# Start of a fused attention and mixer kernel: first constants and loads dealt anew to two DMA queues, with half a warming matmul less

## The chip, the cores and the metric

One core of a Trainium2 chip runs the kernel. The metric is the device time of one execution in microseconds (us). The kernel before was timed three times: 271.75, 270.02 and 270.61 us, median 270.61 us.

The engines go by their short names: PE (TensorE matmuls) and PEld (its weight loads), DVE (VectorE), ACT (ScalarE), POOL (GpSimd), SP (SyncE). A small q behind a name (SPq, ACTq) means the engine's instruction queue at work, for instance issuing a DMA.

## The reference

Four batches, eight heads, 768 positions, head size 64. Scores are masked by blocks of 32 positions: a block pair counts if it lies next to the diagonal, in the first or last block row or column, or if it was sampled for its row. Then softmax, the product with v, and a mixer over the result.

```python
scores = scale * np.matmul(q, k.transpose(0, 1, 3, 2))
mask = np.abs(blk_i - blk_j) <= window
mask = mask | (blk_i == 0) | (blk_j == 0) | (blk_i == n_blocks - 1) | (blk_j == n_blocks - 1)
for qb in range(n_blocks):
    for kb in sampled_blocks[qb]:
        mask[qb * block:(qb + 1) * block, kb * block:(kb + 1) * block] = True
attn = softmax(np.where(mask, scores, -1e9))
x = np.matmul(attn, v)                     # heads side by side: 4 x 768 x 512
h = x.transpose(0, 2, 1) @ U @ V           # low rank over the positions
u = x + h.transpose(0, 2, 1)
out = u + np.maximum(u @ w_ch1, 0.0) @ w_ch2
```

## The kernel before, in words

Heads are worked on in pairs, 16 in all. For each pair q and k are loaded with positions on the partitions, cast to fp16 and turned by PE, so that the head's 64 features lie on the partitions. In the first four pairs (batch 0) the mask goes into the score matmul itself. A head takes 64 partitions for its features and 24 more for the mask: in q's tile these rows hold a one-hot code of the position's block, in k's tile a bias of 0 or -240 for each block. One matmul then gives score plus bias, ACT takes the exponential, and PE multiplies by v. For later pairs a 0/1 mask is built once (L939, L945) and multiplied in by DVE.

All engines follow an order written out by hand (a word list called PLAN, and ahead of it the start, L243 to L342). Nothing is reordered at run time, so an instruction that waits holds up whatever stands behind it on its engine. DMAs are issued from SP's and ACT's queue. Each takes one of eight semaphores in turn, so a DMA waits until the one eight before it has landed.

The start, which is all that the change touches:

- `first_load(h, n, queue)` (L176, issue at L182) loads head h of pair 0: q for n = 0, k for n = 1. Head 0 comes first. Head 1, the second head, is issued later at the same line.
- `small` (L102 to L105, L245) is one constant for all 128 partitions: the static mask and block numbers `ms` and `iota` (24 rows), and the fp16 identity `id16` that PE needs for every turn.
- `sb` (L246) holds the sampled blocks. From `sb`, `iota` and `ms` DVE works out the bias (L302, L306, L309).
- `one_hot` (L186) loads the 24 one-hot rows into the q tile of a head, `qres[i][mrows[h], h]`. For the first set of tiles (i = 0) it is called twice at L254, each time behind a DVE memset (L253). For the second set (i = 1, used from pair 1 on) it is called in `second_set` (L192).
- `keep_warm(8)` (L300) gives PE eight matmuls of 512 columns on constants while it waits for data.
- Then `first_cast` (L213, DVE: fp32 to fp16), `first_turn` (L227, PE: three matmuls each), `first_row` (L293, copies out of the accumulators by ACT and DVE), `mask_half` (L279, PE: bias times one-hot rows) and `mask_row` (L287).
- The second heads of pair 0 are cast by POOL (L213) and turned by PE at L352, after the first scores (L980, L999). Their rows are copied by DVE at L359.
- `load_v(0)`, `load_qk(1)`, `load_v(1)` (L166, L153) follow on SP's queue, then U (L200), `second_set` (with the copy of the mask rows into `kmask`, L196) and V (L206).

The order of the first turn, which both kernels share but for line numbers (two more in the changed one):

```python
first_cast(0, 0, nc.vector.tensor_copy)     # L301
... neq, a01, bias on DVE ...
first_turn(0, 0)                            # L314
first_row(0, 0, nc.scalar.copy)
first_turn(0, 1)
first_row(0, 1, nc.scalar.copy)
first_cast(0, 1, nc.vector.tensor_copy)
mask_half(0)                                # L319
mask_row(0, 0, nc.vector.tensor_copy, 0, P)
mask_row(1, 0, nc.scalar.copy)
first_turn(1, 0)
```

Of the kernel before, what the change touches and what calls it, by code (L numbers as in the profile page):

```python
# [12 lines left out]
FP32 = mybir.dt.float32  # L13
FP16 = mybir.dt.float16
# [5 lines left out]
P = 128  # L20
# [3 lines left out]
def kernel(  # L24
# [14 lines left out]
    nc = tc.nc  # L39

    B, H, S, D = q.shape
    BLK = 32
    NB = S // BLK
# [9 lines left out]
    MASK_BIAS = -240.0  # L53
# [3 lines left out]
    ii = np.arange(NB)  # L57
    ms_np = (
        (np.abs(ii[None, :] - ii[:, None]) <= 1)
        | (ii[None, :] == 0)  # L60
        | (ii[:, None] == 0)
        | (ii[None, :] == NB - 1)
        | (ii[:, None] == NB - 1)
    ).astype(np.float32)
    cols = np.arange(S)
    blk = ((cols % P) * T + cols // P) // BLK
    ohT_np = (blk[None, :] == ii[:, None]).astype(np.float16)
    small_np = np.zeros((P, NB + 1 + P // 2), np.float32)
    small_np[:NB, :NB] = (ms_np - 1.0) * -MASK_BIAS
    small_np[:NB, NB] = ii  # L70
    small_np[:, NB + 1 :] = np.eye(P, dtype=np.float16).view(np.float32)

    small_dr = nc.inline_tensor(small_np, name="small_const")
    ohT_dr = nc.inline_tensor(ohT_np, name="one_hot_const")

    consts = ctx.enter_context(tc.tile_pool(name="consts", bufs=1))
    wpool = ctx.enter_context(tc.tile_pool(name="wpool", bufs=1))
# [21 lines left out]
        ring["psc"] += 1  # L99
        return PS[:, (0, 3)[ring["psc"] % 2] :][:, 0:2]  # L100

    small = consts.tile([P, NB + 1 + P // 2], FP32)  # L102
    ms = small[0:NB, 0:NB]
    iota = small[0:NB, NB : NB + 1]
    id16 = small[:, NB + 1 :].bitcast(FP16)  # L105
    sb = consts.tile([P, NB, 3, 2], I32)
    vts = [consts.tile([P, H, T, DV], FP16, name=f"vt{i}") for i in range(2)]
    NEST = 16
# [3 lines left out]
    res = consts.tile([P, 4, 2, S], FP16, name="res")  # L112
    qres = [res[:, i] for i in range(2)]
    kres = [res[:, 2 + i] for i in range(2)]
    drows = [slice(0, D), slice(D, P)]
    mrows = [slice(D, D + NB), slice(0, NB)]
    hid = consts.tile([P, 2, 16, HS], FP16, name="hid")
# [58 lines left out]
    def first_load(h, n, queue):  # L176

        src, nm = ((q, "qld"), (k, "kld"))[n]
        if h == 0:
            lds[nm] = ldpool.tile([P, 2, T, D], FP32, tag="ld" + nm, name=nm)  # L180
            sts[0, nm] = stpool.tile([P, T, 2, D], FP16, tag="st" + nm, name="st" + nm)
        queue.dma_start(  # L182
            out=lds[nm][:, h], in_=src[0, h].rearrange("(p t) d -> p t d", t=T)
        )

    def one_hot(i, h):  # L186
        nc.sync.dma_start(out=qres[i][mrows[h], h, :], in_=ohT_dr.ap())

    warm = nc.const_aps.tensor(1.0, [P, 512], mybir.dt.bfloat16)
    bias = consts.tile([P, 2, D], FP16)  # L190

    def second_set():  # L192
        for h in range(2):
            one_hot(1, h)
            nc.sync.dma_start(out=kres[1][mrows[h], h, :], in_=kres[0][mrows[h], h, :])
        nc.sync.dma_start(out=kmask[mrows[0], :], in_=kres[0][mrows[0], 0, :])  # L196

# [13 lines left out]
    def first_cast(h, n, copy):  # L211
        nm = ("qld", "kld")[n]
        copy(out=sts[0, nm][:, :, h], in_=lds[nm][:, h])  # L213
# [20 lines left out]
    with tc.manual_schedule(  # L234
# [7 lines left out]
    ):  # L242
        first_load(0, 0, nc.sync)  # L243
        first_load(0, 1, nc.sync)
        nc.scalar.dma_start(out=small, in_=small_dr.ap())  # L245
        nc.scalar.dma_start(  # L246
            out=sb[0:NB].rearrange("k z r w -> k (z r w)"),
            in_=sampled_blocks.bitcast(I32)
            .rearrange("z r -> (z r)")[None, :]
            .broadcast_to([NB, NB * 6]),  # L250
        )
        for h in (1, 0):
            nc.vector.memset(qres[0][(slice(D, P), slice(0, D))[h], h, :], 0.0)  # L253
            one_hot(0, h)  # L254
        nc.vector.memset(bias, 0.0)
        for h in range(2):
            nc.vector.memset(kres[0][(slice(D, P), slice(0, D))[h], h, :], 0.0)
        for n in range(2):
            first_load(1, n, nc.sync)
        for tile_ in (qres[1], kres[1]):  # L260
            nc.gpsimd.memset(tile_.bitcast(FP32), 0.0)
        for vt in vts:
            nc.gpsimd.memset(vt[:, :, :, D : D + 1], 1.0)
        first = consts.tile([P, 1], FP32)
# [1 line left out]
            out=first, in_=nc.const_aps.tensor(1.0, [P, 1], FP32), func=AF.Exp  # L266
# [3 lines left out]
        def keep_warm(n, cols=512):  # L270
            for _ in range(n):
                nc.tensor.matmul(  # L272
                    pw[:, 0, 0:cols], warm[:, 0:P], warm[:, 0:cols], start=True, stop=True
                )
# [17 lines left out]
        def first_row(n, c, copy, lo=0, hi=HS):  # L292
# [4 lines left out]

        neq = consts.tile([P, NB, 3], FP32)
        a01 = consts.tile([P, NB], FP32)
        keep_warm(8)  # L300
        first_cast(0, 0, nc.vector.tensor_copy)  # L301
        nc.vector.tensor_tensor(  # L302
            out=neq[0:NB], in0=sb[0:NB, :, :, 0],
# [3 lines left out]
            out=a01[0:NB], in_=neq[0:NB], axis=mybir.AxisListType.X, op=ALU.min  # L307
        )
        nc.vector.scalar_tensor_tensor(  # L309
            out=bias[0:NB, :, 0:NB], in0=a01[0:NB, None].broadcast_to([NB, 2, NB]),  # L310
# [28 lines left out]
        load_v(1)  # L339
        load_mix_u()  # L340
        second_set()
        load_mix_v()  # L342

# [840 lines left out]
```

## Time and profile before

| | |
|---|---|
| median of three runs | 270.61 us (270.02 to 271.75) |
| the profiled execution | 270.01 us, its span 268.2 us |
| PE busy | 262.4 us, 98% of the span |
| DVE, ACT, POOL busy | 232.5, 202.7, 72.7 us |
| PE busy in 0 to 4, 4 to 8, 8 to 12 us of the span | 3.22, 3.50, 3.81 us |
| DMA rate in the same stretches | 133, 268, 290 GB/s |

The span is the time between the first and the last instruction of the program. The profiled execution's own time is 1.8 us longer than its span. The page gives shares over the whole span. What happens in the first microseconds is seen in the timeline, which lists instructions by start, duration, engine, source line and operands, and in brackets how long the engine had been idle and what released it.

### The profile page before, as it was taken

Reading aid. Unit: us, or ns where it says so; the run is one execution under the profiler, and the core shown is the slowest. Engines: PE = TensorE matmul, PEld = TensorE weight load, DVE = VectorE, ACT = ScalarE, POOL = GpSimd, SP = SyncE. Lnnn points to the kernel's source line nnn. Section 1 sums busy time; section 2 is a strip of 40 time slices with the busy share of each in tenths; the row PEclk is TensorE's granted clock in tenths of the full one; section 3 lists DMA queues with packets and bytes.
Section 4 is the critical chain, followed back from the end, with each engine's and each line's share of the span. In section 5 each row is a group of like instructions: output and inputs, shape, how many; then the busy total and the mean of one; then the engine's idle time right before and its main releaser. Section 6 shows DMA issues by size and latency. Waiting matters only on the chain.

```text
span 268.2 us, 7303 instructions
## 1 busy us (share of the span) xinstructions
PE 262.4 (98%) x3006; PEld 182.4 (68%) x3006; DVE 232.5 (87%) x477; ACT 202.7 (76%) x265; POOL 72.7 (27%) x98
## 2 busy tenths in 40 slices
PE   8899999999999999999999999999999999999995
PEld 3677775555577778565666887555667788666884
DVE  5789988988999998868588997688998999999993
ACT  4999998897989667788898857788997944789200
POOL 4669006944462570070606160000000000000000
PEclk9999999999999999999999999999999999999999
DMA  6799997999999999897938997610200116400024
GB/s 192 245 324 263 207 235 123 113 135 144 189 146 133 117 103 111 284 98 89 90 39 67 106 109 139 223 34 13 51 0 2 42 42 117 159 2 0 2 98 137
DMA packets 88720, 31.66 MB, mean 118 GB/s; under 512 B 77104, under 2 KB 85840, under 8 KB 88688
## 3 DMA queue, kind: packets, MB, share of 16 engines
q0 software_dynamic: 49728, 10.10, 48.4%
q1 hardware_dynamic: 38492, 20.86, 33.6%
q8 instruction: 23, 0.38, 0.6%
q10 hardware_dynamic: 468, 0.26, 0.4%
q14 instruction: 9, 0.07, 0.1%
HBM read 27.67 MB, written 6.29 MB: 127 GB/s over the span
## 4 chain that ended last, share of the span: by engine, by line
PE 73%; DMA 12%; DVE 7%; ACT 2%; POOL 2%; issue 1%; SPq 0%; DVEq 0%; POOLq 0%; ACTq 0%
PE ps L760 32%; PE ps L685 17%; DMA w2t<-in_moe_w_ch_dram 9%; PE ps L414 9%; PE ps L1030 7%; DMA vld<-in_v_dram 2%; PE ps L999 2%; ACT est L1007 2%; PE ps L980 1%; DVE est L1045 1%; PE ps L272 1%; DMA qpl<-stqld 1%; PE ps L665 1%; DVE xf L551 1%; DVE res L969 1%
## 5 line engine op out<-in xcount | busy, mean ns | idle before, releaser
L1039 ACT ACTIVATE est<-ps 128x1536 f16<-128x1536 f32 x72 | 100.6, 1450 | 18.8 <-PE ps L1030 18.7
L685 PE MATMUL ps<-uT,w1t 128*128 128x384 f16 x384 | 70.2, 326 | 0.0
L1045 DVE TENSOR_TENSOR est<-est,mask 128x1440 f16<-128x1440 f16 x72 | 63.4, 903 | 0.6 <-ACT est L1039 0.2
L685 PEld LDWEIGHTS <-w1t 128*128 128x128 f16 x384 | 35.6, 97 | 26.6 <-issue 6.8
L414 PEld LDWEIGHTS <-est 128*128 128x128 f16 x1152 | 40.4, 97 | 7.0 <-issue 3.3
L414 PE MATMUL ps<-vt,est 128*128 128x65 f16 x1152 | 43.3, 193 | 0.2 <-DVE xf L551 0.2
L760 PEld LDWEIGHTS <-hid 128*128 128x128 f16 x358 | 34.0, 98 | 6.6 <-issue 1.6
L697 ACT ACTIVATE hid<-ps 128x384 f16<-128x384 f32 x63 | 29.7, 496 | 4.8 <-PE ps L685 4.3
L1030 PE MATMUL ps<-qpl,kpl 64*128 64x512 f16 (+1 forms) x288 | 31.7, 325 | 0.0
L139 POOL DMA_DIRECT2D stqld<-in_q_dram x20 | 16.3, 820 | 55.9 <-DMA qpl<-stqld 54.4
L760 PE MATMUL ps<-w2t,hid 128*128 128x256 f16 x238 | 31.1, 273 | 0.0
L879 DVE TENSOR_TENSOR xf<-xf,ps 128x256 f32<-128x256 f32 x63 | 25.4, 416 | 4.1 <-PE ps L760 3.7
L699 DVE TENSOR_SCALAR hid<-ps 128x384 f16<-128x384 f32 x33 | 18.3, 555 | 8.7 <-PE ps L685 8.0
L760 PEld LDWEIGHTS <-sums 128*128 128x128 f16 x216 | 20.1, 98 | 4.4 <-issue 1.0
L989 ACT ACTIVATE est<-ps 128x768 f16<-128x768 f32 x30 | 22.5, 812 | 0.1
L1030 PEld LDWEIGHTS <-kpl 64*128 64x128 f16 x288 | 12.3, 94 | 14.3 <-issue 9.1
L760 PE MATMUL ps<-res,sums 128*128 128x256 f16 x144 | 19.4, 273 | 0.0
L634 ACT CAST xh<-xf 128x384 f16<-128x384 f32 x24 | 11.0, 510 | 10.0 <-DVE xf L630 10.0
L551 DVE TENSOR_TENSOR xf<-ps,rcp 128x384 f32<-128x384 f32 x32 | 17.7, 554 | 0.8
L139 POOL DMA_DIRECT2D stkld<-in_k_dram x20 | 16.3, 819 | 1.9 <-issue 0.8
L139 POOL DMA_DIRECT2D vt<-in_v_dram x20 | 16.3, 820 | 0.0
L760 PE MATMUL ps<-res,hid 128*128 128x256 f16 x120 | 15.9, 273 | 0.0
(121 smaller groups left out, 339.3 us busy)
## 6 DMA issues: line engine op xcount, KB each, us to landing
out_dram<-xf SPq DMA_DIRECT2D x18, 256.0 KB, 2.4
vld<-in_v_dram SPq DMA_DIRECT2D x6, 384.0 KB, 6.3
w1t<-in_moe_w_ch_dram POOLq DMA_DIRECT2D x4, 512.0 KB, 8.3
w2t<-in_moe_w_ch_dram POOLq DMA_DIRECT2D x4, 512.0 KB, 12.1
qld<-in_q_dram SPq DMA_DIRECT2D x5, 384.0 KB, 3.7
kld<-in_k_dram SPq DMA_DIRECT2D x5, 384.0 KB
stqld<-in_q_dram POOLq DMA_DIRECT2D x20, 96.0 KB, 3.9
stkld<-in_k_dram POOLq DMA_DIRECT2D x20, 96.0 KB, 4.2
```

Of the source, the lines that this page charges most:

```text
L139: nc.gpsimd.dma_start(out=dst[:, h], in_=src[b, 2 * hp + h].rearrange("(p t) d -> p t d", t=T),)
L414: nc.tensor.matmul(pav[:, sc, :], est[:, n, sc * P : (sc + 1) * P], vts[b % 2][:, 2 * hp + h, g, 0 : D + 1], start=(g == 0 and sc == 0), s ...
L551: nc.vector.tensor_tensor(out=dst, in0=pav[:, :, 0:D], in1=rcp[:, :, None].broadcast_to([P, T, D]), op=ALU.mult,)
L685: nc.tensor.matmul(pt, w1t[:, cc, jj * P : (jj + 1) * P], bts[b].uT[:, cc, c * HS : (c + 1) * HS], start=(cc == 0), stop=(cc == NCC - 1), ...
L697: nc.scalar.activation(out=dst, in_=pt, func=AF.Relu)
L699: nc.vector.tensor_scalar_max(out=dst, in0=pt, scalar1=0.0)
L760: nc.tensor.matmul(acc[key], lhsT, rhs, start=(first and i == 0), stop=(i == len(pairs_) - 1), skip_group_check=True,)
L879: nc.vector.tensor_add(out=x, in0=x, in1=acc[a, b, tau])
L989: lambda: nc.scalar.activation(out=dst, in_=ps, func=AF.Exp, scale=0.125),
L1030: nc.tensor.matmul(units[h][:, u * S + lo : u * S + hi], kT[drows[h], g * P : (g + 1) * P], qT[drows[h], lo:hi], start=True, stop=True, sk ...
L1039: nc.scalar.activation(out=both[h], in_=units[h].rearrange("p (g n) -> p g n", g=2), func=AF.Exp, scale=0.125,)
L1045: lambda: nc.vector.tensor_mul(out=masked(both[h]), in0=masked(both[h]), in1=masked(mask[:, 2 * j : 2 * j + 2, :]),),
```

## The change

The constant `small` is split. Mask constants and one-hot rows become one constant of 32 rows, `hot`, loaded by ACT's queue as the first DMA there. It lands in place: its first 768 columns of fp16 are the one-hot rows of head 1 of the first q tile, and the rest lies in rows of the second q tile that pair 1's data overwrite later. The identity becomes a constant of its own, the third DMA on SP's queue. The one-hot rows of head 0 are no longer loaded: DVE copies the lower 64 rows of head 1 to the upper 64 of head 0, ahead of the first cast. The second set's one-hot rows are copied from the first set's by DMA. The second heads of pair 0 go from SP's queue to ACT's, behind `sb` and ahead of the table load for the exponential. The memsets are cut to the rows that need them. The last of the eight warming matmuls has 256 columns instead of 512.

```diff
-    small_np[:NB, :NB] = (ms_np - 1.0) * -MASK_BIAS
-    small_np[:NB, NB] = ii
-    small_np[:, NB + 1 :] = np.eye(P, dtype=np.float16).view(np.float32)
-    small_dr = nc.inline_tensor(small_np, name="small_const")
-    ohT_dr = nc.inline_tensor(ohT_np, name="one_hot_const")
+    NROW = 32
+    hot_np = np.zeros((NROW, S // 2 + NB + 1), np.float32)
+    hot_np[:NB, : S // 2] = (blk[None, :] == ii[:, None]).astype(np.float16).view(np.float32)
+    hot_np[:NB, S // 2 : S // 2 + NB] = (ms_np - 1.0) * -MASK_BIAS
+    hot_np[:NB, S // 2 + NB] = ii
+    hot_dr = nc.inline_tensor(hot_np, name="hot_const")
+    id_dr = nc.inline_tensor(np.eye(P, dtype=np.float16), name="identity_const")
...
+    id16 = consts.tile([P, P], FP16, name="id16")
+    hot = res.rearrange("p a b s -> p (a b s)")[:, S : 2 * S + 2 * NB + 2].bitcast(FP32)
+    ms = hot[0:NB, S // 2 : S // 2 + NB]
+    iota = hot[0:NB, S // 2 + NB :]
...
-    def one_hot(i, h):
-        nc.sync.dma_start(out=qres[i][mrows[h], h, :], in_=ohT_dr.ap())
+    def second_hot(h):
+        nc.sync.dma_start(out=qres[1][mrows[h], h, :], in_=qres[0][mrows[h], h, :])
     def second_set():
         for h in range(2):
-            one_hot(1, h)
+            second_hot(h)
             nc.sync.dma_start(out=kres[1][mrows[h], h, :], in_=kres[0][mrows[h], h, :])
         nc.sync.dma_start(out=kmask[mrows[0], :], in_=kres[0][mrows[0], 0, :])
...
         first_load(0, 0, nc.sync)
         first_load(0, 1, nc.sync)
-        nc.scalar.dma_start(out=small, in_=small_dr.ap())
+        nc.sync.dma_start(out=id16, in_=id_dr.ap())
+        nc.scalar.dma_start(out=hot[0:NROW], in_=hot_dr.ap())
         nc.scalar.dma_start(
             out=sb[0:NB].rearrange("k z r w -> k (z r w)"),
...
-        for h in (1, 0):
-            nc.vector.memset(qres[0][(slice(D, P), slice(0, D))[h], h, :], 0.0)
-            one_hot(0, h)
+        nc.vector.memset(qres[0][NROW:D, 1, :], 0.0)
         nc.vector.memset(bias, 0.0)
         for h in range(2):
-            nc.vector.memset(kres[0][(slice(D, P), slice(0, D))[h], h, :], 0.0)
+            nc.vector.memset(kres[0][drows[1 - h], h, :], 0.0)
         for n in range(2):
-            first_load(1, n, nc.sync)
+            first_load(1, n, nc.scalar)
         for tile_ in (qres[1], kres[1]):
-            nc.gpsimd.memset(tile_.bitcast(FP32), 0.0)
+            for h in range(2):
+                nc.gpsimd.memset(tile_[drows[1 - h], h, :].bitcast(FP32), 0.0)
...
-        keep_warm(8)
+        keep_warm(7)
+        keep_warm(1, 256)
+        nc.vector.tensor_copy(out=qres[0][drows[1], 0, :], in_=qres[0][drows[0], 1, :])
         first_cast(0, 0, nc.vector.tensor_copy)
```

More of the change, by code (lines that the diff above doesn't have):

```diff
@@ L66 @@
     blk = ((cols % P) * T + cols // P) // BLK
-    ohT_np = (blk[None, :] == ii[:, None]).astype(np.float16)
-    small_np = np.zeros((P, NB + 1 + P // 2), np.float32)
-    small_np[:NB, :NB] = (ms_np - 1.0) * -MASK_BIAS
-    small_np[:NB, NB] = ii
-    small_np[:, NB + 1 :] = np.eye(P, dtype=np.float16).view(np.float32)
-    small_dr = nc.inline_tensor(small_np, name="small_const")
-    ohT_dr = nc.inline_tensor(ohT_np, name="one_hot_const")
+    NROW = 32
[5 more added lines that the diff above has]
+    id_dr = nc.inline_tensor(np.eye(P, dtype=np.float16), name="identity_const")
     consts = ctx.enter_context(tc.tile_pool(name="consts", bufs=1))
@@ L100, in psc2 @@
         return PS[:, (0, 3)[ring["psc"] % 2] :][:, 0:2]
[L102 to L105, printed above, removed]
+    id16 = consts.tile([P, P], FP16, name="id16")
     sb = consts.tile([P, NB, 3, 2], I32)
```

## The prediction

> **What bounds the kernel now.** I read the page first: PE is busy for 262.4 us of a span of 268.2, and nothing in the change takes work off PE but half of one warming matmul. So the change can only move the moment at which the real work starts. Then the chain of waits in order of time, at its start:
>
> ```profile
> 0.78 3.57 PE ps L272 x8
> 4.35 0.47 PE ps L227 x3
> 4.82 0.02 issue
> 4.84 0.85 ACT res L293 x2
> 5.69 0.46 ACT res L287
> ```
>
> The span begins with warming on PE, then three matmuls of the first turn of q (L227), then ACT's copies (L293, L287) back to back. DVE copies, PE scores and exponentials follow, and up to 34 us the chain names no DMA. Then the timeline, for what these few steps wait on:
>
> ```profile
> 0.74 0.39 SPq L182 DMA_DIRECT2D qld<-in_q_dram  x1
> ...
> 0.78 3.57 PE L272 MATMUL ps<-const-bfloat16-1.0 128*128 128x512 bf16 x8 [0.78 <-PEq L1168]
> ...
> 1.20 0.41 SPq L182 DMA_DIRECT2D kld<-in_k_dram  x1
> ...
> 1.85 1.28 ACT L265 ACT_TABLE_LOAD   x1 [1.85 <-issue]
> ...
> 2.49 0.37 SPq L182 DMA_DIRECT2D qld<-in_q_dram  x1
> ...
> 3.38 0.43 SPq L166 DMA_DIRECT2D vld<-in_v_dram  x1
> 3.47 0.36 DVE L213 CAST stqld<-qld 128x384 f16<-128x384 f32 x1 [0.52 <-DMA qld<-in_q_dram]
> ...
> 4.28 0.60 PEld L227 LDWEIGHTS <-stqld 128*64 128x64 f16 x6 [0.84 <-DVE a L306]
> 4.28 0.77 PE L227 MATMUL ps<-small,stqld 128*64 128x128 f16 x6
> ...
> 4.38 0.34 DVE L213 CAST stkld<-kld 128x384 f16<-128x384 f32 x1
> 4.84 0.85 ACT L293 CAST res<-ps 64x384 f16<-64x384 f32 x2 [1.49 <-PE ps L227]
> ...
> 5.24 0.36 PEld L227 LDWEIGHTS <-stkld 128*64 128x64 f16 x6 [0.17 <-issue]
> ...
> 5.79 0.50 POOL L213 CAST stqld<-qld 128x384 f16<-128x384 f32 x1 [3.18 <-DMA qld<-in_q_dram]
> ...
> 13.63 0.10 PEld L939 LDWEIGHTS <-kmask 128*128 128x128 f16 x1
> ```
>
> Three things are to be seen. q lands just before 3.47, and its cast ends at 3.83. PE does not take it up then: the eighth warming matmul occupies it, and the first weights go in at 4.28 (the releaser named there, L306, is not the one: the compiled order waits for the cast alone). From 4.84 ACT runs without a gap. So the start is set by the warming, not by a DMA.
>
> The trace's semaphore records give the landings, by issue: q 3.45 (issued 0.74), small 3.22 (0.74), sb 3.65 (1.13), k 4.09 (1.20), one-hot rows 4.68 and 5.24 (1.65 and 2.14), second q 5.74 (2.49), second k 6.24 (2.90), first v 8.36 (3.38), kmask 13.59 (10.27).
>
> **The change part by part.** I set the sum against the profiled execution: 270.01 us, of which 268.2 are the span and 1.8 lie around it and are left as they are. It stands 0.60 below the median of the three runs.
>
> Warming. Single rows of L272 start 0.427 us apart, so half a matmul is 0.21 us. The first weights went in 0.56 after the eighth had started (3.715 to 4.275); with a half-length eighth they could go in at 4.06. The cast's semaphore at 3.84 allows it. This is worth -0.21 us if the identity is there.
>
> Identity. It was in small, landed at 3.22. Now it is third on SP's queue, issued where the one-hot rows were (1.65), so its packets stand behind q's and k's. Lower bound: k's landing, 4.09, plus eight packets per engine at small's 0.022 us, that is 4.27. The one-hot rows in the same place landed at 4.68, held up by packets of 0.1 to 0.8 us where q's took 0.065; the identity comes from a fresh constant as they did. Upper bound: 4.68 plus 0.52, if each of its eight packets lets one of the second q's, 0.065 us, go ahead, that is 5.20. The second q now comes from ACT's queue about 1.85, and by the 1.0 us from small's issue to its first packet it is active from 2.9, while k's and the identity's packets run. I take 4.27 plus half of 0.52, 4.53, near the one-hot landing, and 0.04 to the matmul: the first turn starts at 4.57, 0.29 later than now. Single rows of L227 start 0.107 apart up to 4.81 and 0.055 apart from 5.24 (the page's PEclk row shows 9 in every slice but the spacing gives the slow start away), so the late turn runs partly in the faster clock and gets back some 0.07. ACT's first copy then starts at about 5.06 instead of 4.84: +0.22 us. The 0.21 from warming is covered by this wait and not to be had in addition.
>
> In row and rule: sb's 24 packets on ACT's queue ran between 2.55 and 3.13, among q's and k's packets from SP's. The Trainium skill (DMA: Bandwidth & Descriptors, Issuing engines are not separate DMA queues) says that DMAs of different issuers share the same engines and interleave, so that a second issuer saves only issue time. This trace agrees. Without any sharing the identity would land at 4.27 and the sum would be 0.0 instead of +0.2.
>
> DVE. One memset of 0.378 us goes (with its gap 0.5), so the memsets end near 2.46 instead of 2.96. A copy of 64x768 fp16 comes, between SBUF rows. No such row exists; bounds are 0.353 (L810, 768 fp16 elements, one input) and 0.561 (L359, the same shape from PSUM). I take 0.35, as L810 also stays within SBUF. It waits for hot, first on ACT's queue as small was (landed 3.22), with two packets per engine instead of eight. If hot lands at 3.0 the copy ends at 3.35, hidden by q's landing at 3.45. If hot lands as small did, the copy ends at 3.57 to 3.78; then it delays the q cast by 0.1 to 0.33, and the cast ends at 3.95 to 4.16. Behind the copy in DVE's queue stand that cast, the bias (three instructions) and the k cast. All this is still ahead of the identity at 4.53, so I cost it at 0; should the identity be early, up to 0.15 comes back here.
>
> ACT. Its two issues more (0.37 and 0.43 as SP's, plus gaps) move the table load from 1.85 to about 2.7, and it ends with its test at 4.2. The first copy needs ACT at 4.84 or later: hidden by 0.6. Upper bound, if the issues took twice as long, +0.2.
>
> SP. Two one-hot issues and two second heads go, one identity comes: the first v issues near 2.1 instead of 3.38, and q of pair 1 near 3.0 (it waits for hot's semaphore) instead of 3.85. In the chain nothing waits for those up to 34 us. The nearest is kmask, landed 13.59, with PE's weights at 13.63 in the last timeline line, after a gap under 0.1. Gain 0 to 0.08, taken as 0. k may land at 4.5 instead of 4.09; its cast ran from 4.38 to 4.72 and PE took it at 5.24, so 0.4 of cover remains.
>
> POOL, second heads and second set. Its two memsets of 0.737 become four; by the 0.419 of L335's 128x384 rows they take 1.7 instead of 1.4. POOL then idles until 5.79 for the second q (3.18 in the line above), so it is hidden. The second heads land about a microsecond earlier, but PE turns them at 8.27 behind scores (L999). The second set's rows come from SBUF instead of memory, and the copies for k in the same place remain. No gain and no loss on the path.
>
> Sum: +0.22, on 270.01 about 270.2; for a median run 270.6 plus 0.2, 270.8. A shift of the start passes through: the DMA stretch of the chain from 34.7 us on is issued behind DVE's work at 33.1, so it moves along.
>
> **The rivals.**
> 1. The identity is no obstacle (the transfers are hidden anyway). For it: k's first engines reported at 3.64, so most of the identity may be in by 4.0. Against it: an engine serves a queue in order, and k's last two reported at 4.02 and 4.09. Then the first turn starts between 4.06 and 4.28: -0.21 to 0, a median of 270.4 to 270.6.
> 2. The other side: the fast clock comes late. PE's matmuls changed from 0.107 to 0.055 us per 128 columns between 4.81 and 5.24, after unbroken work from 0.78. If the wait for the identity leaves PE idle for half a microsecond ahead of that change, and the change falls away, PE stays slow for another such stretch, some 3.4 to 4 us. In 4.9 to 8.6 the chain has the k turn (0.33), two mask halves (0.16 each), the first score (0.32) and L999 (0.82); doubled, they add 1.8, of which ACT's unbroken work covers about 0.6. Price +1.2 on top of +0.2: 272.0. It decides when the first turn starts later than about 4.6 and the gap counts as idleness. Against it: four of the 4.1 us ahead of the change would still be work.
> The Trainium skill (TensorE: Matmul & The Clock Gate, What's actually happening) describes a free-running window of about 3.4 us that has to be busy. By that rule the change needs a busy window, and a gap inside it could cost one window; no run here shows a gap yet.
> 3. The identity lands at 5.2: the first turn starts 0.95 later, of which the faster clock returns 0.16: +0.8, 271.4.
>
> **How the numbers follow.** Forecast (identity lands between 4.3 and 4.9): 0.50. Rival 1: 0.33. Rival 2: 0.09. Rival 3: 0.08. The time is the forecast's, 270.8. The forecast's own range is 270.6 to 271.2. The median of three runs can be off by about 0.8, since the three before span 1.7. From rival 1's 270.4 less 0.8 the range starts at 269.6; it ends at rival 2's 272.0. About 1% (2.7 us) is what a measurement of this kernel can tell from no change. Every case lies within it: same 0.94, slower 0.04 (rival 2 with more than its price), faster 0.02.
>
> **What would show it.** In the timeline of the changed kernel: PE's first L227 weights (4.06 if warming bounds, 4.5 or later if the identity does, and then with PE idle after warming); the start of ACT's first L293 copy, which carries the whole effect; the DVE copy's place against q's landing; the table load ending by 4.3; the spacing of L227 rows of k (0.055, or 0.107 for rival 2). The prediction is wrong if the first copy starts before 4.8, or if the time moves by more than that copy does, which would mean that something after the start has changed.

## The result, and the profile after

The changed kernel takes 273.95 us (median of six runs, 272.35 to 274.89). The kernel before, run beside it on the same chip, takes 270.94 (six runs, 270.02 to 271.75). The ratio is 1.0113, with a 95% interval of 1.0081 to 1.0144: 3.0 us slower, above the predicted range. The profiled execution took 274.45 us, and its span is 4.4 us longer than that of the kernel before.

First the page of the changed kernel: the span, and the busy time of each engine with its share and its number of instructions.

```profile
span 272.7 us, 7303 instructions
...
PE 265.0 (97%) x3006; PEld 184.1 (68%) x3006; DVE 232.4 (85%) x477; ACT 203.1 (74%) x265; POOL 72.8 (27%) x100
```

PE works on as many instructions as before. It is busy for 2.6 us longer and idle for 1.9 us longer (7.7 of 272.7 instead of 5.8 of 268.2). Most of both lies at the start, as the chain of waits of the changed kernel shows from 1.66 us on, in order of time (start, duration, what).

```profile
1.66 3.98 DMA id<-identity_const
5.64 0.04 issue
5.68 0.80 PE ps L227 x6
6.48 0.43 PE ps L279
6.91 0.78 PE ps L227 x6
7.69 0.43 PE ps L279
8.11 2.03 PE ps L982 x6
10.14 1.28 PE ps L1001 x4
```

The chain before began with warming and went to ACT's first copy, naming no DMA. Now SP's issues and then one DMA, the identity, hold its first 5.64 us. Behind it the six matmuls of q's turns, the six of k's, the mask halves and the scores on PE follow one another, where before copies on ACT and DVE stood in the chain. Why PE's work is in the chain is seen from its durations in the timeline of the changed kernel (start, duration, engine, line, operation; in brackets the idle time before and what ended it).

```profile
0.78 3.36 PE L272 MATMUL ps<-const-bfloat16-1.0 128*128 128x512 bf16 x8 [0.78 <-PEq L1170]
...
1.66 0.70 SPq L245 DMA_DIRECT2D id<-identity_const  x1
1.84 0.37 ACTq L182 DMA_DIRECT2D qld<-in_q_dram  x1
...
2.72 1.28 ACT L265 ACT_TABLE_LOAD   x1 [2.72 <-issue]
...
2.90 0.35 DVE L302 COPY res<-res 64x768 f16<-64x768 f16 x1 [0.47 <-DMA res<-hot_const]
...
3.30 0.36 DVE L213 CAST stqld<-qld 128x384 f16<-128x384 f32 x1
...
4.06 0.13 PEld L227 LDWEIGHTS <-stqld 128*64 128x64 f16 x1 [0.62 <-DVE a L308]
...
5.68 0.80 PE L227 MATMUL ps<-id,stqld 128*64 128x128 f16 x6 [1.55 <-DMA id<-identity_const]
...
6.20 0.85 ACT L293 CAST res<-ps 64x384 f16<-64x384 f32 x2 [1.98 <-PE ps L227]
...
8.05 2.10 PE L982 MATMUL ps<-res 128*128 128x384 f16 x6
```

Two things are to be seen. PE takes its weights at 4.06, ends its warming at 4.14 and then idles for 1.55 us: the identity lands at 5.64, and the first turn starts at 5.68. And PE is slow from then on: six score matmuls (L982) take 2.10 us, 0.32 us apart, where the first two in the kernel before took 0.50 and the next four 0.81, 0.16 apart once under way. The clock records in the trace say the same: full speed from 4.83 us before, from 12.97 now. The page's PEclk row reads 9 in every slice of both kernels, so it doesn't show this; the spacing of equal matmuls does.

The stretches between the changes of clock last 3.41 us or a multiple of it in every run here (shown below). Counted back from 12.97 in steps of 3.41, these are two of them in the changed kernel (stretch, its length, PE's busy time and rows, PEclk, DMA share, GB/s):

```profile
2.74:6.15 3.41, 1.86 (x9) 1.00 1.00 300
6.15:9.56 3.41, 3.41 (x17) 1.00 1.02 365
```

The gap lies in the first one, which has PE busy for 1.86 us only. The second one has no gap that the profile shows, and yet full speed comes neither at 9.56 nor before 12.97. It begins with the turns and mask halves, up to 8.05, and has scores for the last 1.5 us. So the gap as such explains one lost stretch of the two. That a stretch of turns and mask halves does not bring full speed is met again in b_one_hot below.

Followed along PE, row against the same row of the kernel before, the delay is 1.41 us at the first turn, 2.1 to 2.5 at the matmuls of L1001, 3.6 at 14 us, and keeps between 3.5 and 3.6 up to 100 us. It is 4.37 from 113 us on; the larger part of the last 0.8 is a wait for a transposing DMA, which the trace of before doesn't have there. This is the changed kernel's timeline on PE:

```profile
113.71 0.32 PE L687 MATMUL ps<-uT,w1t 128*128 128x384 f16 x1 [0.37 <-DMA uT<-xh]
```

So, in this pair of executions, of 4.4 us the late identity makes 1.36 by itself (ACT's first copy starts at 6.20 instead of 4.84), the slow clock 2.2 (3.59 less 1.36, taken as the clock's because the shift alone passes through in a_warm12 below), and something later 0.8.

### The profile page after: what moved, and what is told of

Its sections match the earlier page's. It is cut to its first block, busy times and chain, and to the rows that moved or that the text cites. A ratio compares the mean times of both kernels' runs of the same rounds, so it can differ in the third digit from the quotient of the medians.

```text
span 272.7 us, 7303 instructions
## 1 busy us (share of the span) xinstructions
PE 265.0 (97%) x3006; PEld 184.1 (68%) x3006; DVE 232.4 (85%) x477; ACT 203.1 (74%) x265; POOL 72.8 (27%) x100
## 4 chain that ended last, share of the span: by engine, by line
PE 85%; DVE 6%; ACT 4%; DMA 2%; issue 1%; SPq 0%; DVEq 0%; ACTq 0%
PE ps L762 30%; PE ps L687 23%; PE ps L416 11%; PE ps L1032 9%; PE ps L982 4%; PE ps L1001 3%; ACT est L1041 2%; ACT est L1009 2%; DMA id<-identity_const 1%; DMA uT<-xh 1%; DVE est L1047 1%; PE ps L667 1%; DVE xf L553 1%; DVE hid L723 1%; ACT hid L699 1%
## 5 line engine op out<-in xcount | busy, mean ns | idle before, releaser
L881 DVE TENSOR_TENSOR xf<-xf,ps 128x256 f32<-128x256 f32 x63 | 25.3, 414 | 4.5 <-PE ps L762 3.7
```

The costliest lines, as they stand in the source:

```text
L881: nc.vector.tensor_add(out=x, in0=x, in1=acc[a, b, tau])
```

## The experiments

The theory after the result: the identity lands 1.1 us later than forecast because it stands third on SP's queue while the second heads run from ACT's, and the gap that it opens on PE keeps PE in the slow clock. The rivals: the half warming matmul alone costs the clock, without the identity; the new one-hot scheme with its DVE copy; the place in the queue alone, or the second heads on ACT alone; chance, that is the moment at which an execution meets the clock.

The numbers are collected here, and each experiment refers to its row. "Late transfer" is the landing that PE waited for, from the trace's semaphore records; the two rows with brackets are those where PE waited for something else. "Copy" is the start of ACT's first copy. "Full clock" is from the clock records. "Row 592" is by how much the 592nd PE row behind the warming is later than in the kernel before, where it starts at 51.72. These columns are from one profiled execution each; the median is over n runs, and the ratio is against the kernel before on the same chip (270.94 for the changed kernel, 270.1 to 270.2 for the experiments), with its 95% interval.

| kernel | late transfer | copy | full clock from | row 592 | median (n) | ratio |
|---|---|---|---|---|---|---|
| before | none (q 3.45) | 4.84 | 4.83 | 0 | 270.94 (6) | 1 |
| changed | identity 5.64 | 6.20 | 12.97 | +3.59 | 273.95 (6) | 1.0113 (1.0081 to 1.0144) |
| a_again | identity 6.15 | 6.55 | 4.59 to 8.00, then 11.42 | +2.67 | 273.59 (1) | none |
| a_warm8 | identity 6.11 | 6.67 | 11.96 | +3.34 | 274.25 (5) | 1.0151 (1.0125 to 1.0178) |
| a_warm12 | identity 6.39 | 6.80 | 4.99 | +1.88 | 272.27 (4) | 1.0083 (1.0061 to 1.0106) |
| a_q2sp | identity 5.31 | 5.72 | 4.77 | +0.80 | 273.17 (4) | 1.0104 (1.0051 to 1.0157) |
| a_id2 | k 6.24 | 4.63 | 5.12 to 8.53, then 11.95 | +2.67 | 272.81 (4) | 1.0109 (1.0051 to 1.0167) |
| a_id2_q2sp | k 5.09 | 4.65 | 4.74 | +0.15 | 270.86 (10) | 1.0031 (1.0011 to 1.005) |
| a_idact | sb 4.53 | 4.57 | 4.18 | +0.33 | 272.19 (5) | 1.0079 (1.0059 to 1.0098) |
| a_idpool | identity 4.67 | 5.24 | 9.61 | +1.46 | 272.92 (6) | 1.0099 (1.007 to 1.0128) |
| a_idpool_q2sp | cast of q (identity 4.44) | 5.29 | 4.66 | +0.52 | 271.08 (11) | 1.0058 (1.0029 to 1.0087) |
| b_id3 | identity 4.48 | 5.03 | 5.28 | +1.11 | 270.17 (10) | 1.0005 (0.9979 to 1.003) |
| b_q2act | one-hot 5.27 | 4.84 | 5.24 | +0.37 | 270.49 (10) | 1.001 (0.9992 to 1.0029) |
| b_id3_q2act | identity 5.57 | 5.98 | 3.59 to 7.00, then 10.41 | +1.88 | 271.94 (7) | 1.0073 (1.0046 to 1.01) |
| b_warm5 | q 3.45 | 4.45 | 9.28 | +0.99 | 271.12 (8) | 1.0041 (1.002 to 1.0063) |
| b_warm75 | one-hot 5.20 | 4.63 | 5.24 | +0.25 | 270.54 (12) | 1.0009 (0.9985 to 1.0033) |
| b_one_hot | none | 4.63 | 9.66 | +1.19 | 271.62 (12) | 1.0042 (1.0017 to 1.0066) |

The profiled executions of b_id3 (272.91 us) and of a_q2sp (271.15) are the slowest and the fastest of their runs, so their row 592 doesn't stand for the median. Landings, too, differ between executions: the identity's in the four profiles with the changed kernel's transfers lie between 5.64 and 6.39.

**Warm through the wait (a_warm12).** The changed kernel, with PE kept at work until about 5.6.

```diff
-        keep_warm(7)
-        keep_warm(1, 256)
+        keep_warm(12)
```

> The changed kernel with twelve full warming matmuls, so that PE works until about 5.3 us, and the late identity stays late (5.64). Theory G (the identity comes 1.4 us late, and the 1.5 us in which PE then idles also keep the clock slow until 13 us, for another 2.2 us): the L227 rows start 0.055 us apart, the first ACT copy stays near 6.1, and the time falls by 2.0 to 2.5 us, to about 271.7 us. Rival D (the slow clock is chance, or the loss comes from the DMAs alone): the time stays within 0.5 us of the changed kernel, 273.5 to 274.5 us.

The identity landed even later here, at 6.39, and yet the kernel is only 2.1 us above the kernel before. The same kernel with eight warming matmuls, a_warm8, is 4.1 above it, and the intervals of the two ratios don't meet. The timeline of a_warm12:

```profile
0.78 4.82 PE L272 MATMUL ps<-const-bfloat16-1.0 128*128 128x512 bf16 x12 [0.78 <-PEq L1169]
...
6.44 0.49 PE L227 MATMUL ps<-id,stqld 128*64 128x128 f16 x6 [0.84 <-DMA id<-identity_const]
...
6.80 0.85 ACT L293 CAST res<-ps 64x384 f16<-64x384 f32 x2 [2.58 <-PE ps L227]
...
7.12 0.52 PE L227 MATMUL ps<-id,stkld 128*64 128x128 f16 x6
```

The six matmuls of q's turns take 0.49 us and those of k's 0.52, where the changed kernel's took 0.80 and 0.78: PE is in the full clock. Row 592 is late by 1.88, ACT's first copy by 1.96: a pure shift, with no clock cost. The time is 0.6 us above the 271.7 expected, as the copy is 0.7 later than the 6.1 expected. That separates the two parts of the loss. The direct part of a late identity passes through whole; the clock part goes when PE has work.

**Identity second, k third (a_id2), and the second heads back on SP (a_q2sp).** One edit each on the changed kernel.

```diff
# a_id2
-        first_load(0, 1, nc.sync)
         nc.sync.dma_start(out=id16, in_=id_dr.ap())
+        first_load(0, 1, nc.sync)
# a_q2sp
         for n in range(2):
-            first_load(1, n, nc.scalar)
+            first_load(1, n, nc.sync)
```

> The changed kernel with the identity issued second on SP's queue, ahead of k, and nothing else moved. Theory G: the identity lands at 3.4 to 3.8, PE takes up the first turn at about 4.06 right after the half-length warming matmul, the clock is fast by 5, and the time is that of the kernel before or up to 0.5 us less, 270.2 to 270.9 us. Rival D (the other moves, second heads on ACT's queue above all, cost the time): at least 1.5 us slower than the kernel before, 272.3 us or more.

The identity landed at 4.02 and the first turn of q ran at 4.06, as early as warming allows. But k, now third, landed at 6.24 instead of 3.82. The timeline of a_id2:

```profile
4.06 0.85 PE L227 MATMUL ps<-id,stqld 128*64 128x128 f16 x6
...
6.26 0.36 DVE L213 CAST stkld<-kld 128x384 f16<-128x384 f32 x1 [1.65 <-DMA kld<-in_k_dram]
...
6.68 0.52 PE L227 MATMUL ps<-id,stkld 128*64 128x128 f16 x6 [1.38 <-DVE stkld L213]
```

The same gap, 1.4 us, opens one step later, and the trace's clock falls back. The time expected, 270.2 to 270.9, was missed by two microseconds (272.81). So it isn't the identity, or its small packets, alone that is late: here k is, in the same place. These are the windows of PE in a_id2 (stretch, its length, busy time and rows, PEclk, DMA share, GB/s), cut where the clock records change:

```profile
1.71:5.12 3.41, 3.41 (x14) 1.00 0.77 201
5.12:8.53 3.41, 1.89 (x13) 1.00 1.02 354
8.53:11.95 3.42, 3.34 (x18) 0.50 0.69 226
11.95:15.36 3.41, 2.90 (x48) 1.00 0.51 142
```

PE was released for one stretch of 3.41 us, was busy for only 1.89 of it, and got half the clock (the 0.50 in the third line) for the next. (The first line reads 1.00 although matmuls in it are still 0.107 apart: ahead of the first release the column is not to be trusted.)

> The changed kernel with the second heads of pair 0 back on SP's queue, behind the identity, which stays third. Theory G with sharing (the identity's small packets each let one of the second heads' packets go ahead): the identity lands at 4.2 to 4.5 instead of 5.64, PE idles for 0.2 to 0.5 us only, and the time is 270.5 to 271.5 us. Without sharing (the identity is slow by itself, as a fresh constant): it lands after 5.2 and the time stays above 273 us.

With the second heads on SP the identity landed at 5.31, still third and still late. The 4.2 to 4.5 expected from sharing was missed. What came is the other case, after 5.2 and above 273 us (273.17), by which the identity is slow by itself; b_id3 below speaks against that, where it landed at 4.48 alone. There is a gap on PE of 1.2 us by the wait table of a_q2sp (engine, line, what it waited for: total, times, longest):

```profile
PE ps L227 <- DMA id<-identity_const: 1.2, 1, 1.2
```

In this execution the clock came at 4.77 all the same, and row 592 lost only 0.80, the copy's 0.88. The median is no better than the changed kernel's, so the other executions of a_q2sp lose more; which way they do isn't in a profile.

**Fewer warming matmuls alone (b_warm5, b_warm75).** On the kernel before, 5 instead of 8, and the change's own 7.5.

```diff
-        keep_warm(8)
+        keep_warm(5)          # b_warm5
+        keep_warm(7)          # b_warm75, these two lines
+        keep_warm(1, 256)
```

> The kernel before with five warming matmuls instead of eight: PE idles from about 3.0 to 3.9, and no DMA is moved. Theory G: this gap of 0.9 us ahead of the usual change of clock is enough to keep the clock slow for at least one window more, and the time rises by 1 to 2.5 us, to 271.8 to 273 us, though the first turn starts 0.3 us earlier. Rival D (the clock does not mind the gap): the time falls by 0 to 0.4 us.

The first copy started 0.39 us earlier, and the kernel is about 1 us slower (271.12 against 270.17): PE idled from 3.07 to 3.89, and full clock came at 9.28. So a gap at the start can cost the clock without any of the changed transfers.

> The kernel before with the last warming matmul at 256 columns, nothing else. If the warming bounds the start, the first turn starts at 4.06 instead of 4.28 and the time falls by 0.1 to 0.2 us (the mask halves still wait for one-hot rows that land at 4.7); if the clock minds even this, up to 0.5 us slower.

The half matmul alone costs nothing that can be measured, 1.0009 (0.9985 to 1.0033). It gives nothing either, although the first copy started 0.21 us earlier, because the first mask half then waited for the one-hot rows (5.20).

**The two moves apart and together (b_id3, b_q2act, b_id3_q2act).** On the kernel before: the identity alone in third place on SP, the second heads alone on ACT, and both. Eight warming matmuls in all three.

```diff
# b_id3
+        nc.sync.dma_start(out=id16, in_=id_dr.ap())   # third on SP, taken out of small
# b_q2act
-            first_load(1, n, nc.sync)
+            first_load(1, n, nc.scalar)
# b_id3_q2act: both
```

> The kernel before with the identity alone taken out of small and issued third on SP's queue; all other transfers as before, the second heads still behind it on SP's queue, eight warming matmuls. Theory P (what stands third on SP's queue lands about a microsecond after k, whatever it is): the identity lands at 4.8 to 5.4, the first turn starts there, 0.5 to 1.1 us late, and the time rises by 0.5 to 3 us, by how the idle time falls in the clock's windows. Theory S (the second heads on ACT's queue hold it up): it lands by 4.5, and the time is within 0.3 us of the kernel before.

> The kernel before with the second heads of pair 0 alone moved to ACT's queue. Identity and mask constants stay first on ACT's queue. If the late identity is the whole loss, the first turn starts at 4.28 as before and the time is within 0.4 us of the kernel before, unless the one-hot rows, third on SP's queue, now land after 5.0 and hold up the mask halves: then 0.5 to 1 us slower. If the second heads on ACT's queue cost by themselves: 1.5 us slower or more.

> The kernel before with both moves together, the identity third on SP's queue and the second heads on ACT's queue; small without the identity, one-hot loads and eight warming matmuls as before. Each move alone cost 0.0 and 0.3 us. Theory C (they cost together: the second heads run beside the identity, it lands at 5.2 to 5.9, and PE idles for over 0.9 us, which also costs clock): 1.0 to 3.5 us above the kernel before. Theory A (the two effects only add up): 0.2 to 0.5 us above it, and the loss of the changed kernel comes from something else, such as the new table of mask constants.

The identity alone lands at 4.48 and the first turn starts at 4.52, within 0.05 of the prediction's numbers; the time doesn't move. The second heads alone cost 0.3 us, within the interval. Together they cost 1.7. The wait tables of b_id3 and of b_id3_q2act:

```profile
PE ps L227 <- DMA id<-identity_const: 0.2, 1, 0.2
```

```profile
PE ps L227 <- DMA id<-identity_const: 1.6, 1, 1.6
```

From 0.2 to 1.6 us for the same instruction: with the second heads active from ACT's queue, the third transfer of SP's queue lands at 5.57 instead of 4.48. The windows of b_id3_q2act, cut at its clock records, show the second part of the price, a stretch with 1.83 of 3.41 us busy and half the clock behind it:

```profile
3.59:7.00 3.41, 1.83 (x16) 1.00 0.90 272
7.00:10.41 3.41, 3.41 (x12) 0.50 0.94 318
10.41:13.82 3.41, 3.22 (x47) 1.00 0.40 122
```

Row 592 is late by 1.88, the copy by 1.14, so the clock makes 0.74 in this execution. These three runs are the main finding: two edits that cost 0 and 0.3 alone cost 1.7 together.

They have limits. 1.7 is a part of the 3.0 us of the changed kernel, and the rest isn't traced to one edit. And in the changed kernel neither move is harmless alone: with the second heads taken back (a_q2sp) or the identity put second (a_id2) it stays at 1.0104 and 1.0109, and only both together (a_id2_q2sp, below) bring it to 1.0031. Both b_id3 and a_q2sp have the identity third and the second heads on SP's queue, and yet it lands at 4.48 in the one and at 5.31 in the other. One difference between them is that the second q is issued at 2.97 in the first, behind two loads of one-hot rows, and at 2.13 in the second. So it may be the early issue of the second heads, and not the queue, that counts; no run separates the two.

**Identity on ACT (a_idact), and both cures at once (a_id2_q2sp).** On the changed kernel.

```diff
# a_idact: second heads on SP, and
         nc.scalar.dma_start(out=hot[0:NROW], in_=hot_dr.ap())
+        nc.scalar.dma_start(out=id16, in_=id_dr.ap())     # ahead of sb
# a_id2_q2sp: the edits of a_id2 and a_q2sp
```

> The changed kernel with the identity second on ACT's queue (behind the mask constants, ahead of the sampled blocks) and the second heads on SP's queue behind k. Theory P: the identity lands by 3.6, the first turn starts at 4.06, and the time is that of the kernel before or up to 0.4 us less (269.8 to 270.3 beside 270.2), unless the sampled blocks, now third on ACT's queue, land after 4.6 and hold up the mask bias. Theory N (the identity is slow because its table is touched for the first time): it lands after 4.3 here too.

The identity landed at 3.94. Now sb stood third on its queue and came at 4.53, and the bias with it; PE's wait table for a_idact:

```profile
PE ps L279 <- DVE bias L311: 0.6, 1, 0.6
```

Here, too, the third on its queue delays what needs it. The time expected, 269.8 to 270.3, was missed. The profiled execution was the fastest of five, at 270.71; the median, 272.19, isn't explained by it.

> The changed kernel with the identity second and k third on SP's queue, and the second heads behind k on SP's queue, so that nothing on ACT's queue runs beside k. In the run with the second heads on ACT's queue k landed at 6.24. Theory P (third place): k still lands after 5.0, and the k turn with it; the time is 0.5 to 2 us above the kernel before. Theory S (sharing): k lands at 4.2 to 4.5, and the time is within 0.3 us of the kernel before.

This is the best arrangement of the changed kernel: the identity at 4.03, k third at 5.09 (6.24 with the second heads on ACT), a gap of 0.37, 270.86. Both signs of theory P came, k after 5.0 and 0.5 to 2 us of loss. It is still 0.3% above the kernel before (1.0011 to 1.005).

**The one-hot scheme alone (b_one_hot).** On the kernel before: 7.5 warming matmuls, one one-hot load and one memset less, head 0's rows by a DVE copy, here behind the cast of k.

```diff
-        for h in (1, 0):
-            nc.vector.memset(qres[0][(slice(D, P), slice(0, D))[h], h, :], 0.0)
-            one_hot(0, h)
+        nc.vector.memset(qres[0][drows[0], 1, :], 0.0)
+        one_hot(0, 1)
...
+        nc.vector.tensor_copy(out=qres[0][drows[1], 0, :], in_=qres[0][drows[0], 1, :])
         mask_half(0)
```

> The kernel before with three parts of the change that keep the identity where it was: half a warming matmul less, one one-hot load less at the start, and head 0's one-hot rows copied by DVE (behind the k cast). The second heads stay on SP's queue and are issued about 0.5 us earlier. Expected: first turn at 4.06, time 0.1 to 0.5 us below the kernel before. If the copy on DVE holds up the mask rows, it is within 0.2 us of it.

Five runs took 270.5 to 270.7 and seven 271.6 to 273.0. The 0.1 to 0.5 us of gain that was expected was missed. The profiled one (271.56) has no gap over 0.2 us on PE, and its clock still came only at 9.66. The timeline of b_one_hot shows what PE did in the window 2.84 to 6.25 that failed to release it:

```profile
0.78 3.36 PE L271 MATMUL ps<-const-bfloat16-1.0 128*128 128x512 bf16 x8 [0.78 <-PEq L1169]
...
4.07 0.85 PE L227 MATMUL ps<-small,stqld 128*64 128x128 f16 x6
...
4.85 0.50 PE L278 MATMUL ps<-res,bias 24*128 24x384 f16 x1
...
5.27 0.85 PE L227 MATMUL ps<-small,stkld 128*64 128x128 f16 x6
...
6.05 0.50 PE L278 MATMUL ps<-res,bias 24*128 24x384 f16 x1
```

Only 1.2 us of that window is warming. The rest are turns with weights of 128 by 64 and mask halves with weights of 24 by 128, where the warming has 128 by 128. That this is why they didn't count is argued, not shown: no run here varies the width alone.

**The changed kernel once more (a_again), and with eight full warming matmuls (a_warm8).**

> The changed kernel once more, for a second profile of it. Theory G: the identity lands after 5 again, PE idles for over a second of a microsecond window's third, and the time is 272 to 275 us by where the clock's windows of 3.4 us fall; the record of the clock shows either a late first full stretch or a full stretch that is broken by one slow window. If the late identity was a chance of one execution, it lands before 4.7 here.

> The changed kernel with eight full warming matmuls, only the half taken off put back. PE then idles from about 4.3 until the identity, 0.2 us less. If the half matters only through that idle time, the time stays within 0.7 us of the changed kernel, 273.2 to 274.2; if it is what tips the clock, it falls by 1 us or more.

Both repeat the result: the identity at 6.15 and 6.11, gaps of 2.05 and 1.8 us. The half matmul given back doesn't help (274.25). In a_again PE had been released at 4.59, inside the gap, and lost the clock from 8.00 to 11.42; in a_warm8 it was not released until 11.96. This is its stretch with most of the warming:

```profile
1.73:5.14 3.41, 2.62 (x7) 1.00 0.66 180
```

2.62 us of it are warming and nothing else, and they did not release the clock. The clock's share (row 592 less copy) is 2.2, 1.0 and 1.5 us in the three profiles of this start, by where the windows fell.

**Identity on POOL's queue (a_idpool, a_idpool_q2sp).** As the first DMA there; in the second also with the second heads on SP and eight warming matmuls.

```diff
-        nc.sync.dma_start(out=id16, in_=id_dr.ap())
+        nc.gpsimd.dma_start(out=id16, in_=id_dr.ap())
```

> The changed kernel with the identity as the first DMA on POOL's queue instead of the third on SP's; all else as changed, the second heads on ACT's queue and the half-length warming matmul too. If the identity's place is what costs, it lands before 4.0 here, the first turn starts at 4.06 to 4.2, PE idles for less than 0.5 us in one piece, and the time falls from 273.9 to within 1 us of the kernel before (270.2 to 271.2). If the other moves cost by themselves, 272 us or more.

> The same with the second heads back on SP's queue behind k and eight full warming matmuls: of the change remain the mask constants with the one-hot rows, DVE's copy, and the rows copied for the second set. First turn at 4.28, time within 0.4 us of the kernel before; if these parts help, 0.2 to 0.4 us below it, and it is the version that beats both.

The first missed: its other case came, 272 us or more, by which the other moves cost by themselves. The identity came at 4.67, a microsecond earlier than in the changed kernel, but full clock only at 9.61, and the median is 272.92. The timeline of a_idpool also shows a new cost:

```profile
1.22 0.70 POOL L245 DMA_DIRECT2D id<-identity_const  x1 [0.77 <-POOLq L1170]
...
1.96 1.98 POOL L261 MEMSET res<- 64x384 f32 x4
...
3.63 0.99 DVE L213 CAST stqld<-qld 128x384 f16<-128x384 f32 x1
...
4.71 0.81 PE L227 MATMUL ps<-id,stqld 128*64 128x128 f16 x6 [0.57 <-DMA id<-identity_const]
```

POOL's memsets come later here and run beside DVE's cast of q, which takes 0.99 us instead of 0.36. With the second heads on SP and the eighth matmul whole, the clock came at 4.66 and the median is 271.08, 0.6% over the kernel before, which also missed. But there the first turn didn't wait for the identity (4.44). The timeline of a_idpool_q2sp:

```profile
3.30 1.15 DVE L301 COPY res<-res 64x768 f16<-64x768 f16 x1 [0.86 <-DMA res<-hot_const]
...
4.89 0.52 PE L227 MATMUL ps<-id,stqld 128*64 128x128 f16 x6 [0.55 <-DVE stqld L213]
```

DVE's copy of the one-hot rows took 1.15 us instead of 0.35, beside POOL's later memsets, and held up the cast of q. So this run is no clean test of the rest of the change: it mends two faults and adds one. What is seen is that no version here beats the kernel before.

## Why the prediction was wrong, step by step

**Warming, first weights at 4.06: right.** They went in at 4.06, and the gain was covered by the wait for the identity, as the prediction had it.

**Identity, 4.53 between 4.27 and 5.20: this step failed.** It landed at 5.64, and at 6.11 to 6.39 in three more profiles with the same transfers (a_again, a_warm8, a_warm12). The upper bound had two parts, and both were too small. It started from one landing of the one-hot rows in that place, 4.68; in four profiles with the second heads on SP's queue (before, b_warm5, b_warm75, b_one_hot) these rows landed anywhere from 4.43 to 5.20. And it gave each of eight packets one second-head packet ahead of it, 0.52 in all. The identity landed at 4.48 in b_id3 and, with the second heads from ACT, at 5.57 in b_id3_q2act; k in third place at 5.09 and 6.24; the identity in the changed kernel at 5.31 (a_q2sp) and 5.64 to 6.39. So in these pairs the sharing goes with 0.3 to 1.2 us, each landing from one execution. In the changed kernel the term was +1.36, not +0.22. The prediction wrote that a second issuer saves only issue time (the Trainium skill, DMA: Bandwidth & Descriptors, Issuing engines are not separate DMA queues); the traces agree that the queues share.

**The clock, rival 2, +1.2 with a chance of 0.09: this step failed too; the right mechanism, made too small and taken as another case.** The place that decided was the one named: a first turn later than 4.6, with a gap behind the warming. PE gaps of 1.4 us and more cost the clock in five profiles (the changed kernel, a_again, a_warm8, a_id2, b_id3_q2act), one of 0.8 did so in b_warm5. One of 0.6 in a_idpool stands beside a late clock too, but b_one_hot's clock was as late without a gap. 1.2 in a_q2sp and 0.8 in a_warm12 did not, as the gap fell across a window's edge there or behind the release. The price was 0.7 to 2.2 us against 1.2 forecast, as up to two windows of 3.41 us are lost, not one (in the changed kernel the second of them had no gap). Above all, rivals 2 and 3 were added up as alternatives. They are one chain: the late identity of rival 3 opens the gap that rival 2 needs. Rival 3's +0.8 plus rival 2's extra 1.2 would have put 2.0 on the median, near 272.6, and a range up to there with a fair chance on the chain. With the sizes measured in the three profiles of this start (1.4 to 1.8 direct, 1.0 to 2.2 clock) the sum at row 592 is 2.7 to 3.6, about the 3.0 of the medians.

The Trainium skill (TensorE: Matmul & The Clock Gate, What's actually happening) describes a free-running window of about 3.4 us that must be busy. Here full and half stretches last 3.41, 259.41, 262.83 and 266.24 us, 1, 76, 77 and 78 times 3.413, and they start at another moment in each execution: on the window the traces agree. Being busy was not enough, though: 3.41 of 3.41 us on PE did not release the clock in the changed kernel (6.15 to 9.56) or in b_one_hot (2.84 to 6.25).

**DVE: right.** The copy took 0.35 (2.90 to 3.25), the 0.35 taken, and the cast of q followed at 3.30, ahead of where it stood before. **ACT: right.** The table load moved to 2.72 and ended at 4.00. **SP, POOL: right on the path.** The first v was issued at 2.4 and nothing at the start waited for it; POOL's memsets ended at 3.0 and it waited until 5.47. The second heads were to land about a microsecond earlier; the second q came 0.3 earlier (5.42) and the second k 0.4 later (6.61), which nothing on the path felt.

**"A shift of the start passes through": right up to 100 us.** The delay keeps between 3.5 and 3.6 from 14 us to there; then 0.8 comes on top, which the prediction didn't have.

**The rule for being wrong held.** The first copy was not early, but the time moved by 4.4 in the profiled pair where that copy moved by 1.36, which said that more than the start's shift had changed. It was mostly the clock.

**What stays open.** It stays open why the third transfer can be late even without the second heads on ACT's queue. All queues move little just then, and in the kernel before as well. These are its windows between 3.0 and 4.2 us (last number GB/s):

```profile
3.00:3.40 0.40, 0.40 (x3) 1.00 1.02 377
3.40:3.80 0.40, 0.40 (x3) 1.00 0.57 169
3.80:4.20 0.40, 0.40 (x2) 1.00 0.71 111
```

In a_q2sp the rate is 142, 97 and 118 GB/s from 3.4 to 4.6, and the identity's packets are spread over 3.2 to 5.0; in b_id3 it is 124 and 197 up to 4.2, and the last packet starts at 4.1. In the changed kernel the identity's 256-byte packets take only 0.018 us each, but trickle in from 3.5 to 5.05. So the slump isn't made by the second heads on ACT's queue; what makes it, and what sets its length, isn't shown. Whether place and freshly loaded constant both matter was not separated.

What the rest of the change costs isn't traced either: with the identity no longer third and the second heads on SP, a_id2_q2sp is 0.3% and a_idact 0.8% over the kernel before, and b_one_hot, which moves neither, is 0.4% over. The kernel before has a median of 270.94 in the six runs beside the changed kernel and of 270.1 to 270.2 in the 76 later ones, so the loss may be nearer 3.8 us than 3.0. The later 0.8 us differs from profile to profile (0.2 to 0.8 in this start). About 0.2 of it is a wait of PE for DVE (L881 there) at 101.85, which stands in the profiles of the changed kernel, of all its variants and of b_one_hot, and in none of the other kernels; the rest was traced no further than the wait at 113 us.

How much work, and of what width, a window needs is bounded only: 2.77 of 3.41 us of warming released the clock in a_q2sp and 2.62 did not in a_warm8; 2.84 with narrow turns did not in a_idpool, nor did 3.41 of 3.41 in b_one_hot. The busy time goes by modelled ends of matmuls: by their starts, at 0.107 us for 128 columns, PE has some 0.5 us less work than 3.41 in the changed kernel's 6.15 to 9.56 (an estimate).

## What to carry to other kernels

At a start, ask what is third in each DMA queue and what runs beside it from the other queue, and price the two together. In the kernel before each alone was nearly free; in the changed kernel taking back one of them didn't bring the time back. Price a PE gap ahead of or just after the release of the clock by the windows that it can lose, and not by its length; a few warming matmuls more (a_warm12) bought that back here. And where one rival's lateness is the condition of another, they are one case, and their prices add.

## What the runs showed of the hardware that was not expected

- A released clock is lost again after one stretch of 3.41 us in which PE is idle for about half of it (busy 1.81 to 1.89, in a_id2, b_id3_q2act and a_again); stretches busy for 2.56 to 2.9 us kept it.
- The times of one kernel fall into groups: of 82 executions of the kernel before, 66 took 269.4 to 270.9 us and 16 took 271.2 to 271.9. The clock's windows start at another moment each time, which would give such groups; no profile was taken of each group to show it.
- A DVE cast of 128x384 took 0.99 us instead of 0.36 while POOL set memory beside it (a_idpool), and a DVE copy of 64x768 took 1.15 instead of 0.35 (a_idpool_q2sp). That the memsets are the cause is not shown: in a_idpool the same copy ran beside them in 0.35.
